# Attention and two feed-forward layers on one core: the last 64 keys of four heads as one unit of the attention

## The chip, the cores and the metric

One core of one Trainium2 chip runs the whole program in a single launch. The metric is the device time of one execution in microseconds; of several executions the median is given, so lower is better. A profile is one further execution with the hardware profiler on, and times inside it are counted from the start of its span.

## The reference

Four batches, twelve heads, 448 tokens, head size 64; all data is float32.

```python
S = q.shape[2]                                   # 448
scores = matmul(q, k.T) / sqrt(64) - log(S)
attn = 1 / (1 + exp(-scores))                    # a sigmoid: no sum over the keys
out = matmul(attn, v)                            # (4, 12, 448, 64)
x = out.transpose(0, 2, 1, 3).reshape(1792, 768)
h = x @ w_in;   g = s * relu(h)**2 + b;                   x = g @ w_out      # 768 -> 2048 -> 768
h = x @ w_in2;  g = max(h, 0) + alpha * min(h, 0);        y = g @ w_out2     # 768 -> 2048 -> 768
```

The weights come as float64 and are turned into float32 on the chip.

## The kernel before

**Two stages.** First the attention, then the two feed-forward layers, each in two passes over half of the tokens. The change touches the attention alone.

**The attention's tiling.** Two heads j = 0, 1 form a head pair, numbered q = 0 to 23. Their keys and queries lie one head on partitions 0 to 63 and the other on 64 to 127, in one tile of 128 x 896 (448 columns of keys, 448 of queries). The 448 keys are cut into chunks c = 0 to 3 of 128, 128, 128 and 64 keys. One chunk of one head pair is a unit; there are 24 x 4 = 96, numbered u in that order. The lists of the program below call the tiles `ga`, since all of the attention's buffers are carved out of tiles that the next stage uses for other things.

**One unit.** `emit_qk` (line 234) multiplies keys by queries. A matmul takes 64 rows of the array (the head size) and 64 of its columns (64 keys), so a chunk of 128 keys is four matmuls, one in each quarter of the array: rows by head j, columns by key half h. `emit_sig` (line 248) applies the sigmoid on ScalarE to both heads at once and writes to SBUF. `emit_av` (line 257) multiplies values by the result: rows are now the 64 keys of half h, columns the 64 outputs of head j, again four matmuls in four quarters; what the two halves give is summed up in two separate PSUM banks of the tile `av`. The last chunk has only half h = 0: two matmuls instead of four in each step, and a sigmoid over 64 partitions.

**The order of the work** is written out by hand (`manual_schedule`): step u issues the key-query matmuls of unit u, the value matmuls of unit u - 2, and the sigmoid of unit u. Each engine runs its own instructions in that order and waits on semaphores. Scores have two PSUM buffers, `av` has two, `sg` five in SBUF, keys-and-queries four, values four.

**Around it.** `emit_x` (line 274), in the step that issues a head pair's last value matmul, sums the two banks: a ScalarE copy of one, then a VectorE add of the other, then for batches 0 and 1 a split in two terms on VectorE, for batches 2 and 3 a store to DRAM (line 289). Sixteen times the first weights are converted from float64: `convert` (line 123), four VectorE operations, in the steps that `conv_step` (line 307) names; it reads a tile `r` that came by DMA (line 120; two buffers), and its result is stored (line 158).

**Transfers.** All are issued by SyncE, in order. In step 4q + 2 the keys, queries and values of head pair q + 3 are loaded (lines 226 and 232), so they stand in SyncE's queue behind whatever earlier steps left there: the store of the last conversion, which waits for VectorE, and the next load of `r`, which waits until the conversion has read its buffer.

Of the kernel before, what the change touches and what calls it, by code (L numbers as in the profile page):

```python
# [11 lines left out]
AF = mybir.ActivationFunctionType  # L12
# [4 lines left out]
P = 128  # L17
# [16 lines left out]
def tile_kernel(  # L34
# [14 lines left out]
    B, NPR, _, SKQ = kq.shape  # L49
    S = SKQ // 2  # L50
    NCH = vt.shape[4]
    D = vt.shape[5]
    NK = NPR
    DM = NK * P
    NFC = w_in1.shape[0]
    QKSCALE = 1.0 / math.sqrt(D)
# [1 line left out]
    T2 = 2 * S  # L58
    NCUT = len(OUT_CUTS)
    PER = NFC + NK * NCUT  # L60
    LAST = S - (NCH - 1) * P

    def pool(name, bufs, **kw):
        return ctx.enter_context(tc.tile_pool(name=name, bufs=bufs, **kw))
# [13 lines left out]
    def acc_tile(name):  # L78
        return ps.tile([P, 2, 512], F32, tag="acc", name=name)

    def av_tile(name):
        return ps_av.tile([P, 2, 512], F32, tag="av", name=name)

    def t_tile(name):
        return tp.tile([P, T2], F32, tag="t", name=name)
# [4 lines left out]
    def split(hi, lo, src, eng_hi):  # L90
        if eng_hi == "A":
            nc.scalar.copy(hi, src)  # L92
        else:
            nc.vector.tensor_copy(hi, src)  # L94
        nc.vector.tensor_tensor(out=lo, in0=src, in1=hi.bitcast(F32), op=ALU.subtract)  # L95

    bias_t = const.tile([P, 1], F32, name="bias_t")
# [25 lines left out]
    def convert(j, w, eng):  # L123

        n = units[j][1]
        v = r64.pop(j)[:, : 2 * n].rearrange("p (n t) -> p n t", t=2)
        lo, hi = v[:, :, 0], v[:, :, 1]
        a = cvp.tile([P, WMAX], U32, tag="cva", name="cva")[:, :n]
        u = w[:, :n].bitcast(U32)

        if eng == "A":
            nc.scalar.activation(a.bitcast(F32), hi.bitcast(F32), AF.Relu, scale=-(2.0**-80))  # L134
        else:
            nc.vector.tensor_scalar(
                out=a.bitcast(F32), in0=hi.bitcast(F32), scalar1=-(2.0**-80), scalar2=0.0,
                op0=ALU.mult, op1=ALU.max,
            )
        nc.vector.scalar_tensor_tensor(  # L140
            out=a.bitcast(F32), in0=hi.bitcast(F32), scalar=2.0**-112, in1=a.bitcast(F32),
            op0=ALU.mult, op1=ALU.max,
        )

        nc.vector.tensor_scalar(
            out=u, in0=lo, scalar1=2.0**-29, scalar2=7.0, op0=ALU.mult, op1=ALU.min
        )
        nc.vector.scalar_tensor_tensor(  # L148
            out=u, in0=a, scalar=3, in1=u,
            op0=ALU.logical_shift_left, op1=ALU.bitwise_or,  # L150
        )
        to_store.append((j, w))

    def store32():
        for j, w in to_store:
            n = units[j][1]
            w32[j] = dram.tile([P, n], F32, tag=f"w{j}", name=f"w{j}")
            nc.sync.dma_start(out=w32[j], in_=w[:, :n])
        to_store.clear()
# [10 lines left out]
    def split_unit(i):  # L170
        if i >= len(uses):
            return
        n = units[uses[i]][1]
        t = whlp.tile([P, 2, WMAX], F32R, tag="whl", name="whl")
        split(t[:, 0, :n], t[:, 1, :n], wraw.pop(i)[:, :n], "A")
        whl[i] = t
# [7 lines left out]
    def next64():  # L184
        if at64[0] < len(order64):
            load64(order64[at64[0]])
            at64[0] += 1
# [4 lines left out]
    def x_tile(kc):  # L192
        x[kc] = xp.tile([P, 2, 2, S], F32R, tag=f"x{kc}", name=f"x{kc}")
        return x[kc]

    def x_store(key, shape_cols, name):
        if key not in x_dram:
            x_dram[key] = dram.tile([P, 2, S], F32, tag=name, name=name)
        return x_dram[key]


    NU = B * NPR * NCH
    kqt, vtt, sct, sgt, avt = {}, {}, {}, {}, {}
    stores = []

# [5 lines left out]
    def buffer(what, cols):  # L211
        first, n = place[what]
        t = ga[first + taken[what] % n]
        taken[what] += 1
        return t[:, WMAX : WMAX + cols]

    def where(u):
        q, c = divmod(u, NCH)
        bb, pr = divmod(q, NPR)
        return q, bb, pr, c  # L220

    def load_kq(q):
        if q < B * NPR:
            bb, pr = divmod(q, NPR)
            kqt[q] = buffer("kq", SKQ)
            nc.sync.dma_start(out=kqt[q], in_=kq[bb, pr])

    def load_v(q):
        if q < B * NPR:
            bb, pr = divmod(q, NPR)  # L230
            vtt[q] = buffer("v", 2 * NCH * D).rearrange("p (j c d) -> p j c d", j=2, c=NCH)
            nc.sync.dma_start(out=vtt[q], in_=vt[bb, pr])

    def emit_qk(u):
        q, bb, pr, c = where(u)
        t = kqt[q]
        sc = acc_tile("sc")
        for h in range(2 if c < NCH - 1 else 1):
            for j in range(2):
                rows = slice(j * D, (j + 1) * D)  # L240
                keys = slice(c * P + h * D, c * P + (h + 1) * D)
                nc.tensor.matmul(  # L242
                    sc[h * D : (h + 1) * D, j, :S], t[rows, keys], t[rows, S:],
                    start=True, stop=True,
                )
        sct[u] = sc

    def emit_sig(u):
        c = u % NCH
        n = P if c < NCH - 1 else LAST  # L250
        sg = buffer("sg", T2).rearrange("p (j s) -> p j s", j=2)
        nc.scalar.activation(  # L252
            sg[:n], sct.pop(u)[:n, :, :S], AF.Sigmoid, bias=bias_t[:n, 0:1], scale=QKSCALE
        )
        sgt[u] = sg

    def emit_av(u):
        q, bb, pr, c = where(u)
        if c == 0:
            avt[q] = av_tile("av")  # L260
        sg = sgt.pop(u)

        for h in range(2 if c < NCH - 1 else 1):
            for j in range(2):
                keys = slice(h * D, (h + 1) * D)
                nc.tensor.matmul(  # L266
                    avt[q][j * D : (j + 1) * D, h, :S],
                    vtt[q][keys, j, c, :],
                    sg[keys, j, :],
                    start=(c == 0),  # L270
                    stop=(c == NCH - 1 - h),
                )

    def emit_x(q):
        bb, pr = divmod(q, NPR)
        av = avt.pop(q)
        t = t_tile("xo")[:, :S]
        nc.scalar.copy(t, av[:, 0, :S])  # L278
        nc.vector.tensor_tensor(out=t, in0=av[:, 1, :S], in1=t, op=ALU.add)  # L279
        if bb < 2:  # L280
            if bb == 0:
                x_tile(pr)
            split(x[pr][:, 1, bb], x[pr][:, 0, bb], t, "V")
        else:
            stores.append((x_store((0, 1, pr), S, f"xa{pr}")[:, bb - 2], t))

    def flush_stores():
        for dst, t in stores:
            nc.sync.dma_start(out=dst, in_=t)
        stores.clear()  # L290
# [13 lines left out]
    nc.sync.dma_start(out=b_t, in_=b.to_broadcast([P, 1]))  # L304
    nc.sync.dma_start(out=al_t, in_=alpha)
    next64()
    conv_step = {4 + (k * 88) // NFC: k for k in range(NFC)}
    for u in range(NU + 2):
        if u < NU:
            emit_qk(u)  # L310
        if u >= 2:
            emit_av(u - 2)
        if u < NU:
            emit_sig(u)
        flush_stores()
        store32()
        if u % NCH == 1 and u > NCH:
            emit_x(u // NCH - 1)
        if u % NCH == 2:
            load_kq(u // NCH + 3)  # L320
            load_v(u // NCH + 3)
        if u in conv_step:
            k = conv_step[u]
            w = ga[k][:, :WMAX]
            convert(k, w, "V")
            wraw[k] = w
            next64()
        if u == NU - 4:
            split_unit(0)
        if u == NU - 1:  # L330
            split_unit(1)
# [126 lines left out]
    for n, st in enumerate(steps):  # L458
        kind, m, p, c, cut = st
# [71 lines left out]
```

## Time and profile before

| what | value |
|---|---|
| median of 3 runs | 1100.8 us (1100.18 to 1102.32) |
| the profiled execution | 1100.52 us, of which its span is 1098.7 us |
| TensorE busy in the span | 1090.1 us (99%) |
| attention: first key-query matmul, first matmul of the next stage | 4.2 us, 150.98 us |
| attention: sigmoids | 96 in 147 us |
| the rest of the span | 151 us to the end, TensorE busy 943.3 of 947 us up to 1098 |

Read it from TensorE: it has no idle time that counts after the first 4.2 us, so what the attention costs is what TensorE's quarters are occupied with, unless somebody makes it wait. The start times of the sigmoids are the best ruler, since each follows its unit's key-query matmuls at once.

### The profile page before, as it was taken

What the parts mean: (1) busy time and instruction counts of PE and PEld (TensorE: products, weight loads), DVE (VectorE), ACT (ScalarE), POOL (GpSimd) and SP (SyncE); (2) the same over time, 40 slices, a digit from 0 to 9 for tenths busy, and PEclk for the clock granted to TensorE, in tenths of its full rate; (3) what the DMA queues carried; (4) which work ended last, traced back from release to release, by engine and by line L of the source; (5) the groups of instructions that cost most, each with busy time, mean ns of one, the idle gap of its engine ahead of it and who ended that gap; (6) DMA issues with size and microseconds to landing.
All of it is one profiled execution on the core that took longest, in us unless ns stands there. A gap on an engine that the chain in (4) does not pass through costs nothing.

```text
span 1098.7 us, 14184 instructions
## 1 busy us (share of the span) xinstructions
PE 1090.1 (99%) x5952; PEld 930.7 (85%) x5952; DVE 449.6 (41%) x567; ACT 433.9 (39%) x519; POOL 0.2 (0%) x4
## 2 busy tenths in 40 slices
PE   8999999999999999999999999999999999999998
PEld 3444469999999999999999999999999999999997
DVE  3664433346455144544333244375552234431110
ACT  6777753334333134342323244453331344431110
POOL 0000000000000000000000000000000000000000
PEclk9999999999999999999999999999999999999999
DMA  6878720004677433344565511146773111122210
GB/s 248 303 266 309 241 111 1 1 11 145 216 212 223 146 99 120 117 137 141 185 211 187 180 53 48 44 118 184 242 220 116 60 58 58 41 65 67 84 55 34
DMA packets 46864, 147.22 MB, mean 134 GB/s; under 512 B 5584, under 2 KB 7120, under 8 KB 46800
## 3 DMA queue, kind: packets, MB, share of 16 engines
q1 hardware_dynamic: 46800, 146.31, 40.9%
q8 instruction: 47, 0.77, 0.3%
q14 instruction: 17, 0.14, 0.0%
HBM read 107.36 MB, written 38.93 MB: 133 GB/s over the span
## 4 chain that ended last, share of the span: by engine, by line
PE 99%; DMA 0%; ACT 0%; issue 0%
PE hps L344 43%; PE ops L344 43%; PE sc L242 7%; PE av L266 7%; DMA ga<-in_kq 0%; ACT o L411 0%
## 5 line engine op out<-in xcount | busy, mean ns | idle before, releaser
L344 PE MATMUL hps<-x,whl 128*128 128x448 f32 x2304 | 474.6, 367 | 0.0
L344 PE MATMUL ops<-g,whl 128*128 128x448 f32 (+1 forms) x2304 | 469.9, 365 | 0.0
L344 PEld LDWEIGHTS hps<-x,whl 128*128 128x128 f32 x2304 | 432.5, 188 | 42.0 <-issue 0.7
L344 PEld LDWEIGHTS ops<-g,whl 128*128 128x128 f32 x2304 | 432.6, 188 | 36.6
L95 DVE TENSOR_TENSOR whl<-wraw,whl 128x768 fp32r<-128x768 f32 (+1 forms) x120 | 108.3, 902 | 272.4 <-ACT whl L92 272.4
L92 ACT CAST whl<-wraw 128x768 fp32r<-128x768 f32 (+1 forms) x120 | 94.5, 787 | 204.3 <-PE ops L344 186.7
L242 PE MATMUL sc<-ga 64*64 64x448 f32 x672 | 143.9, 555 | 4.2 <-DMA ga<-in_kq 4.2
L266 PE MATMUL av<-ga,ga 64*64 64x448 f32 x672 | 142.2, 540 | 0.0
L252 ACT ACTIVATE ga<-sc,bias_t 128x896 f32<-128x896 f32 x96 | 96.6, 1007 | 40.8 <-PE sc L242 28.9
L365 ACT ACTIVATE t<-hps 128x896 f32<-128x896 f32 x32 | 29.4, 918 | 145.1 <-PE hps L344 145.1
L95 DVE TENSOR_TENSOR g<-t,g 128x896 fp32r<-128x896 f32 x64 | 69.9, 1093 | 33.4 <-ACT g L92 32.3
L242 PEld LDWEIGHTS sc<-ga 64*64 64x64 f32 x672 | 44.6, 134 | 44.5 <-issue 34.8
L371 DVE SCALAR_TENSOR_TENSOR t<-n,nal_t,t 128x896 f32<-128x896 f32 x32 | 36.9, 1152 | 104.1 <-ACT n L370 104.1
L266 PEld LDWEIGHTS av<-ga,ga 64*64 64x64 f32 x672 | 44.9, 133 | 40.1 <-issue 39.3
L94 DVE CAST g<-t 128x896 fp32r<-128x896 f32 x32 | 20.1, 627 | 130.8 <-ACT t L366 130.8
L369 ACT ACTIVATE t<-hps 128x896 f32<-128x896 f32 x32 | 29.4, 918 | 93.1 <-PE hps L344 93.1
L140 DVE SCALAR_TENSOR_TENSOR cva<-r,cva 128x768 f32<-128x768 f32 (+1 forms) x68 | 61.7, 907 | 0.6
L92 ACT CAST g<-t 128x896 fp32r<-128x896 f32 x32 | 30.1, 942 | 39.0 <-DVE t L371 39.0
L134 ACT ACTIVATE cva<-r 128x768 f32<-128x768 f32 (+1 forms) x52 | 44.4, 853 | 0.0
L411 ACT COPY o<-ops 128x896 f32<-128x896 f32 x12 | 10.9, 907 | 70.8 <-PE ops L344 57.1
L279 DVE TENSOR_TENSOR xo<-av,xo 128x448 f32<-128x448 f32 x24 | 15.0, 625 | 57.4 <-ACT xo L278 57.3
L148 DVE SCALAR_TENSOR_TENSOR wraw<-cva,wraw 128x640 uint32<-128x640 uint32 (+1 forms) x36 | 31.3, 870 | 1.2
(26 smaller groups left out, 242.9 us busy)
## 6 DMA issues: line engine op xcount, KB each, us to landing
r<-in_w_in SPq DMA_DIRECT2D x32, 768.0 KB, 5.4
wraw<-w SPq DMA_DIRECT2D x60, 384.0 KB, 3.0
r<-in_w_out SPq DMA_DIRECT2D x24, 640.0 KB, 4.8
ga<-in_kq SPq DMA_DIRECT2D x24, 448.0 KB, 6.6
r<-in_w_out SPq DMA_DIRECT2D x12, 768.0 KB, 5.5
w<-wraw SPq DMA_DIRECT2D x24, 320.0 KB, 5.7
wraw<-w SPq DMA_DIRECT2D x24, 320.0 KB, 3.0
ga<-in_vt SPq DMA_DIRECT2D x24, 256.0 KB, 6.8
```

Of the source, the lines that this page charges most:

```text
L92: nc.scalar.copy(hi, src)
L95: nc.vector.tensor_tensor(out=lo, in0=src, in1=hi.bitcast(F32), op=ALU.subtract)
L134: nc.scalar.activation(a.bitcast(F32), hi.bitcast(F32), AF.Relu, scale=-(2.0**-80))
L140: nc.vector.scalar_tensor_tensor(out=a.bitcast(F32), in0=hi.bitcast(F32), scalar=2.0**-112, in1=a.bitcast(F32), op0=ALU.mult, op1=ALU.max,)
L148: nc.vector.scalar_tensor_tensor(out=u, in0=a, scalar=3, in1=u, op0=ALU.logical_shift_left, op1=ALU.bitwise_or,)
L242: nc.tensor.matmul(sc[h * D : (h + 1) * D, j, :S], t[rows, keys], t[rows, S:], start=True, stop=True,)
L252: nc.scalar.activation(sg[:n], sct.pop(u)[:n, :, :S], AF.Sigmoid, bias=bias_t[:n, 0:1], scale=QKSCALE)
L266: nc.tensor.matmul(avt[q][j * D : (j + 1) * D, h, :S], vtt[q][keys, j, c, :], sg[keys, j, :], start=(c == 0), stop=(c == NCH - 1 - h),)
L344: nc.tensor.matmul(dst[:, bk, :c], w[a], mv[m][bk][:, :c], start=first and k == 0, stop=last and k == 2,)
L365: nc.scalar.activation(t3, h, AF.Relu)
L369: nc.scalar.activation(t3, h, AF.Relu)
L371: nc.vector.scalar_tensor_tensor(out=t, in0=n, scalar=nal_t[:, fc : fc + 1], in1=t, op0=ALU.mult, op1=ALU.add)
```

## The change

The units get another order and another last chunk. Two head pairs q (even) and q + 1 now share it: the unit (q, 3) takes the last 64 keys of q in the columns h = 0 and the last 64 keys of q + 1 in the columns h = 1, and q + 1 itself has only chunks 0 to 2. So two head pairs are 4 + 3 = 7 units instead of 8, and there are 84 units, each with four matmuls per step and a sigmoid over 128 partitions. The values' tile holds the last 64 keys twice, on partitions 0 to 63 and 64 to 127 (it did before, the second copy unused), so the h = 1 matmuls of the shared unit read them from the partitions where they are. The sums of the odd pair begin in the shared unit for bank h = 1 and in its chunk 0 for bank h = 0. `emit_x`, the loads and the conversions keep their rules, counted in the new steps: a load of pair q + 3 in the step of (q, 2), the sixteen conversions spread over 76 steps instead of 88.

```diff
-    NU = B * NPR * NCH
+    order = []
+    for q in range(0, B * NPR, 2):
+        order += [(q, c) for c in range(NCH)] + [(q + 1, c) for c in range(NCH - 1)]
+    NU = len(order)
...
-    def where(u):
-        q, c = divmod(u, NCH)
-        bb, pr = divmod(q, NPR)
-        return q, bb, pr, c
+    def tiles(u):
+
+        q, c = order[u]
+        if c == NCH - 1:
+            return [(h, q + h, c * P) for h in range(2)]
+        return [(h, q, c * P + h * D) for h in range(2)]
...
     def emit_qk(u):
-        for h in range(2 if c < NCH - 1 else 1):
+        for h, q, k0 in tiles(u):
             for j in range(2):
                 rows = slice(j * D, (j + 1) * D)
-                keys = slice(c * P + h * D, c * P + (h + 1) * D)
                 nc.tensor.matmul(
-                    sc[h * D : (h + 1) * D, j, :S], t[rows, keys], t[rows, S:],
+                    sc[h * D : (h + 1) * D, j, :S],
+                    kqt[q][rows, k0 : k0 + D],
+                    kqt[q][rows, S:],
                     start=True, stop=True,
                 )
...
     def emit_av(u):
-        for h in range(2 if c < NCH - 1 else 1):
+        for h, q, _ in tiles(u):
+            if q not in avt:
+                avt[q] = av_tile("av")
+            first = c == (NCH - 1 if q % 2 and h else 0)
+            last = c == (NCH - 1 if not q % 2 and not h else NCH - 2)
...
-    conv_step = {4 + (k * 88) // NFC: k for k in range(NFC)}
+    conv_step = {4 + (k * (NU - 8)) // NFC: k for k in range(NFC)}
...
-        if u % NCH == 1 and u > NCH:
-            emit_x(u // NCH - 1)
-        if u % NCH == 2:
-            load_kq(u // NCH + 3)
-            load_v(u // NCH + 3)
+        if u >= 2:
+            q, c = order[u - 2]
+            if c == NCH - 1 - q % 2:
+                emit_x(q)
+        if u < NU and order[u][1] == 2:
+            load_kq(order[u][0] + 3)
+            load_v(order[u][0] + 3)
```

TensorE's instructions at the program's start. `sc` is a score tile, `av` a sum; `ga0` and `ga1` hold keys and queries of pairs 0 and 1, `ga9` and `ga10` their values, `ga4` to `ga8` the sigmoids' results; x4 counts the matmuls. Before:

```order
L242 MATMUL sc_138<-ga0_93 64x448 x4
L266 MATMUL av_143<-ga4_97,ga9_102 64x448 x4
L242 MATMUL sc_151<-ga0_93 64x448 x2
L266 MATMUL av_143<-ga5_98,ga9_102 64x448 x4
L242 MATMUL sc_159<-ga1_94 64x448 x4
L266 MATMUL av_143<-ga6_99,ga9_102 64x448 x4
L242 MATMUL sc_176<-ga1_94 64x448 x4
L266 MATMUL av_143<-ga7_100,ga9_102 64x448 x2
```

The same place with the change:

```order
L245 MATMUL sc_138<-ga0_93 64x448 x4
L271 MATMUL av_143<-ga4_97,ga9_102 64x448 x4
L245 MATMUL sc_151<-ga0_93 64x448 x2
L245 MATMUL sc_151<-ga1_94 64x448 x2
L271 MATMUL av_143<-ga5_98,ga9_102 64x448 x4
L245 MATMUL sc_161<-ga1_94 64x448 x4
L271 MATMUL av_143<-ga6_99,ga9_102 64x448 x4
L245 MATMUL sc_178<-ga1_94 64x448 x4
L271 MATMUL av_143<-ga7_100,ga9_102 64x448 x2
L271 MATMUL av_185<-ga7_100,ga10_103 64x448 x2
```

The two matmuls of pair 0's last chunk and two of pair 1's now fill one score tile, and the matmuls on pair 1's keys begin one step earlier, in the middle of a unit.

SyncE's queue where pair 20 is loaded (its keys and queries go to `ga0`, its values to `ga9`; `r64` is a float64 weight, `w12` a converted one, `xa` a store of a finished sum). Before:

```order
L226 DMA ga3_96<-in_kq 128x896
L232 DMA ga12_105<-in_vt 128x512
L289 DMA xa4_998<-xo_995 128x448
L226 DMA ga0_93<-in_kq 128x896
L232 DMA ga9_102<-in_vt 128x512
L120 DMA r64_1018<-in_w_in1 128x1536
L158 DMA w12_1028<-ga12_105 128x768
```

With the change:

```order
L232 DMA ga3_96<-in_kq 128x896
L238 DMA ga12_105<-in_vt 128x512
L119 DMA r64_993<-in_w_in1 128x1536
L293 DMA xa4_987<-xo_984 128x448
L157 DMA w12_1006<-ga12_105 128x768
L232 DMA ga0_93<-in_kq 128x896
L238 DMA ga9_102<-in_vt 128x512
```

The load of pair 20 stood ahead of the transfers that wait for a conversion and now stands behind them.

## Rows read from the trace of the kernel before

**Rows 1.** The page's head: span; engines' busy time; TensorE's granted clock in 40 slices.
```profile
span 1098.7 us, 14184 instructions
...
PE 1090.1 (99%) x5952; PEld 930.7 (85%) x5952; DVE 449.6 (41%) x567; ACT 433.9 (39%) x519; POOL 0.2 (0%) x4
...
PEclk9999999999999999999999999999999999999999
```

**Rows 2.** The page's chain that ended last: shares of the span by engine.
```profile
PE 99%; DMA 0%; ACT 0%; issue 0%
```

**Rows 3.** Groups by line and shape, first 170 us: busy us, mean ns | idle before.
```profile
L242 PE MATMUL sc<-ga 64*64 64x448 f32 x672 | 143.9, 555 | 4.2 <-DMA ga<-in_kq 4.2
L266 PE MATMUL av<-ga,ga 64*64 64x448 f32 x672 | 142.2, 540 | 0.0
L252 ACT ACTIVATE ga<-sc,bias_t 128x896 f32<-128x896 f32 x72 | 72.6, 1008 | 29.7 <-PE sc L242 17.8 <-PE av L266 10.0 <-ACT xo L278 0.4
...
L252 ACT ACTIVATE ga<-sc,bias_t 64x896 f32<-64x896 f32 x24 | 24.1, 1003 | 11.1 <-PE sc L242 11.1
...
L278 ACT COPY xo<-av 128x448 f32<-128x448 f32 x24 | 12.6, 523 | 0.5 <-PE av L266 0.5
```

**Rows 4.** ScalarE in order of time: units 0, 16, 18 to 20 and 95.
```profile
6.04 1.01 ACT L252 ACTIVATE ga<-sc,bias_t 128x896 f32<-128x896 f32 x1 [3.82 <-PE sc L242]
...
30.18 1.01 ACT L252 ACTIVATE ga<-sc,bias_t 128x896 f32<-128x896 f32 x1 [0.53 <-PE sc L242]
...
33.19 1.01 ACT L252 ACTIVATE ga<-sc,bias_t 128x896 f32<-128x896 f32 x1
34.66 1.00 ACT L252 ACTIVATE ga<-sc,bias_t 64x896 f32<-64x896 f32 x1 [0.46 <-PE sc L242]
36.19 1.01 ACT L252 ACTIVATE ga<-sc,bias_t 128x896 f32<-128x896 f32 x1 [0.53 <-PE sc L242]
...
148.91 1.00 ACT L252 ACTIVATE ga<-sc,bias_t 64x896 f32<-64x896 f32 x1 [0.46 <-PE sc L242]
```

**Rows 5.** TensorE in order of time: unit 20's eight key-query records, others left out.
```profile
34.44 0.55 PE L242 MATMUL sc<-ga 64*64 64x448 f32 x3
...
34.82 0.85 PE L242 MATMUL sc<-ga 64*64 64x448 f32 x4
...
35.51 0.54 PE L242 MATMUL sc<-ga 64*64 64x448 f32 x1
```

**Rows 6.** SyncE in order of time: loads of pair 5 and pair 23.
```profile
26.20 0.38 SPq L226 DMA_DIRECT2D ga<-in_kq  x1
...
131.95 0.33 SPq L120 DMA_DIRECT2D r<-in_w_out  x1
...
133.37 0.40 SPq L226 DMA_DIRECT2D ga<-in_kq  x1
```

**Rows 7.** Issue to landing (last number, us): loads of pairs 5, 16 and 23.
```profile
ga<-in_kq SPq DMA_DIRECT2D x1, 448.0 KB, 6.0
...
ga<-in_kq SPq DMA_DIRECT2D x1, 448.0 KB, 6.8
...
ga<-in_kq SPq DMA_DIRECT2D x1, 448.0 KB, 8.1
```

**Rows 8.** ScalarE in order of time: units 81 and 92.
```profile
127.90 1.01 ACT L252 ACTIVATE ga<-sc,bias_t 128x896 f32<-128x896 f32 x1 [0.50 <-PE sc L242]
...
144.43 1.01 ACT L252 ACTIVATE ga<-sc,bias_t 128x896 f32<-128x896 f32 x1 [0.53 <-PE sc L242]
```

**Rows 9.** DMA in the first 155 us; two windows (last: clock, DMA share, GB/s).
```profile
DMA packets 13983, 40.60 MB, mean 262 GB/s; under 512 B 1936, under 2 KB 3472, under 8 KB 13968
...
100.00:120.00 20.00, 20.00 (x192) 8.84 (x185) 9.50 (x15) 14.69 (x17) 0.00 (x0) 1.00 0.89 319
...
100.00:104.00 4.00, 4.00 (x44) 1.76 (x37) 2.79 (x4) 2.51 (x4) 0.00 (x0) 1.00 1.02 411
```

**Rows 10.** TensorE in order of time: the next stage's first matmuls.
```profile
150.98 5.33 PE L344 MATMUL hps<-x,whl 128*128 128x448 f32 x25
```

## What I predict

> **What bounds the kernel now.** I read the page's head first. TensorE is busy 99% of a span of 1098.7 us at the full granted clock (2.4 GHz of the two levels 1.2 and 2.4) [rows 1], and the chain that ended last is TensorE too, 99% [rows 2]. So time is gained only where TensorE is occupied for less long. The groups by line come next: in the attention the key-query matmuls waited once, 4.2 us at the start for the first load, and the value matmuls never [rows 3]. The two groups' busy times, 143.9 and 142.2 us, overlap almost fully: both run through the same stretch, in different quarters of the array. Hence a group's busy time can't be used as a cost, and a ruler is needed that counts each moment once.
>
> That ruler is the sigmoid, one per unit. Its starts run from 6.04 us (unit 0) to 148.91 us (unit 95) [rows 4]: 142.87 us over 95 steps, 1.504 us a step. The reader is to see that the half unit is not cheaper: unit 18 starts at 33.19, unit 19 (64 partitions, two matmuls instead of four) at 34.66, unit 20 at 36.19, steps of 1.47 and 1.53 us, and four units from 30.18 to 36.19 are 6.01 us [rows 4]. Three full steps and a half one take four full steps. The reason is in the layout: a quarter gets one key-query matmul and one value matmul per unit, and in a half unit the quarter of rows 0 and columns 0 still gets both, while the other quarters get one or none. The fullest quarter sets the pace.
>
> **What the change removes.** It removes 12 of 96 steps. The number of matmuls is the same (24 pairs x 14 of each kind), and each quarter now has the same number. 12 x 1.504 = 18.05 us. From the execution's own 1100.52 us that is 1082.5 us. That execution lies 0.28 us below the median of the runs shown and inside their spread of 2.1 us, so I keep its level. The bound on the shared unit's own step, which no row shows, is from both sides: 1.47 us (the half unit's step, though with half the matmuls) and 3.01 us, two steps (the halves run one after the other). I take 1.504 because it has exactly the four matmuls in four quarters of a full unit, and because the value matmuls of full units already stream four different operands into the four quarters at the pace of 1.504 us; that the two halves of the key-query step now stream different queries is therefore nothing new to the array. Should it behave like the half unit instead, another 0.03 us x 12 = 0.4 us is gained; more than that is excluded, since no quarter can do its two matmuls in less than the fullest quarter takes now.
>
> **What it adds on ScalarE and VectorE.** The sigmoid over 128 partitions takes 1008 ns, over 64 it took 1003 [rows 3]: nothing. ScalarE has per two pairs 7 x 1.008 + 2 x 0.523 = 8.1 us of work in 7 x 1.504 = 10.53 us; before it was 9.1 in 12.03. Its copy still ends ahead of the next sigmoid, as the step after a copy in the trace is no longer than others (30.18 to 36.19 contains one). The sum of a pair must be out of PSUM four steps (6.0 us) after `emit_x` is issued instead of five (7.5 us); against that stand the copy, 0.52 us, and an add that may be behind one conversion. I cost this at nothing; cover gone, it would cost the excess of that sum over 6 us, and I see none within 1.5 us.
>
> **What it moves: the loads' lead.** This is what is late next. A load of pair q + 3 is emitted in the step of (q, 2). Before, its first matmul came 10 steps later, 15.04 us. Now it is 8 steps, 12.03 us (for an odd pair the first use is the shared unit, for an even one there are 3 + 3 + 2 steps), so each load has 3.0 us less. SyncE is in order, so a load behind a conversion loses more. In the new order of steps a conversion falls into the same step as `emit_x`, with a load right behind, twice: step 8 (load of pair 5 in step 9) and step 61 (load of pair 20 in step 62). Behind a waiting key-query matmul on TensorE stand the value matmuls, and the whole stage with them, so such a wait counts in full.
> When is a load needed? Unit 20's first key-query record starts at 34.44 us [rows 5] and its sigmoid at 36.19 [rows 4]: 1.75 us ahead. The second half of the eight records lies between 34.82 and 35.51 [rows 5]; I take 1.25 us ahead.
> Pair 5: before, the same conversion stood in step 9 and the load was issued at 26.20 us [rows 6]; one step earlier is 24.70, and with the landing of 6.0 us [rows 7] the keys are there at 30.70. They are needed in the second half of unit 17: its sigmoid would start at 6.04 + 17 x 1.504 = 31.61, less 1.25 is 30.36. Wait: 0.3 us.
> Pair 20: the same figure of conversion, store and load stood before at pair 23. Unit 81's sigmoid started at 127.90 [rows 8], SyncE issued the weight load, freed by the conversion, at 131.95 and the pair's load at 133.37 [rows 6], 5.47 us after the sigmoid; it landed 8.1 us later [rows 7], at 141.47, and was needed at 144.43 [rows 8] - 1.75 = 142.68. It was 1.2 us early with 11 steps between conversion and use. Now there are 9 (61 to 70): 3.0 us less, 1.8 us late. With the landing of 6.8 us of pair 16 [rows 7], which was loaded behind a conversion too, it is 0.5 us late. Between the ends I take 1.1 us.
> The other loads follow a conversion that VectorE has done earlier, or none. Sum of waits 1.4 us, from 0 (both in time) to 3.5 us (both at the late end, and one more pair of their kind).
>
> **Sum.** 1100.52 - 18.05 + 1.4 = 1083.9 us. The feed-forward stage keeps its order and its work; it starts 16.65 us sooner.
>
> **The rivals.**
> *Transfers set the pace.* The first 155 us move 40.60 MB [rows 9]. Nearly all of it now falls into about 134 us: 303 GB/s instead of 262. In the second half, where finished sums are stored too, two pairs need, by the tiles' sizes, 2 x (448 + 256 + 224) KB and, with a conversion every 76 / 16 = 4.75 steps, 7 / 4.75 weights of 768 + 384 KB: 3.64 MB in 10.53 us, 346 GB/s. For it: the busiest 20 us already show a share of 0.89 at 319 GB/s [rows 9]. Against it: at a share of 1.02 there were 411 GB/s [rows 9], and the mean leaves gaps. If the 40.60 MB went at 319 GB/s and no faster, the last would land at 127 us, just ahead of the stage's end; at 300 GB/s at 135 us, which is 4 to 5 us on top: 1086 to 1093 us with queueing. Chance 0.11.
> The Trainium skill speaks against the change here: its page "DMA: Bandwidth & Descriptors", section "Where 436 GB/s comes from", says that transfers between HBM and SBUF are held by the HBM side at about 358 GB/s a core. By it the 3.64 MB would take 10.2 of 10.53 us, and by the row's 411 GB/s 8.9 us. The trace does not agree with the page as a ceiling; 4 us at 411 GB/s stand against it, so I don't raise the chance for it.
>
> *The change doesn't do what it says.* If the two heads' halves of a shared unit don't run beside each other, each shared step is two: 12 x 1.504 comes back, 1100.5 us; if only the key-query half is held up, half of it, 1091.5 us. Against it is the pace of the value matmuls above. Chance 0.05.
>
> *Slower: every load is late.* With four buffers and loads tied to steps, TensorE's step can't be shorter than an eighth of the time from a load's step to its landing. The latest in the trace is pair 23: step 82's first key-query record, 1.504 - 1.75 us from unit 81's sigmoid, is at 127.65, and the keys land at 141.47, 13.8 us later. If denser traffic made that the rule for all and added to it, the 84 steps would take 84 x T / 8; they are as long as before, and 2.2 us more, at T = 14.0 us. At T = 15 us they take 157.5 us, 13 more than 144.4: 1114 us. Against it: only loads that stand behind a conversion of the same step come near (pair 5: step 10 begins at 6.04 + 10 x 1.504 - 1.75 = 19.33, landing 32.2, 12.9 us), and there are now two such of 24. Chance 0.02.
>
> **Chances.** Forecast with its own range, 1082.2 to 1086: 0.80. Better than that: 0.02. Pace of transfers 0.11, halves one after the other 0.05, slower 0.02. The range is 1082.2 to 1087.5: below lies only 0.02, above it some 0.13. A change under 0.2% (2.2 us) can't be told from none by a measurement of this kernel. Faster is then all of the first three and about half of the fourth, 0.95; same 0.03; slower 0.02.
>
> **What would show it.** Right: 84 sigmoids over 128 partitions, 1.50 us apart through shared units as well; the next stage's first matmul near 134.3 us instead of 150.98 [rows 10]; waits of key-query matmuls for loads of pair 5 at about 30 us and pair 20 at about 110 us, together 1 to 2 us, none elsewhere; VectorE never waiting for a weight load after the first. Wrong: a step of 2 us or more around each shared unit (the halves don't overlap), a wait at most pairs (the transfers set the pace), ScalarE waiting for nothing while TensorE waits for a sigmoid (ScalarE has become the bound), or a granted clock below full anywhere.

## The result, and the profile after

The changed kernel takes 1083.71 us (median of 4 runs, 1081.99 to 1085.06) against 1100.49 us beside it: a ratio of 0.9844, 95% interval 0.9825 to 0.9863. Timed a second time, with the experiments, it took 1082.74 us (5 runs), ratio 0.9833 (0.9820 to 0.9847). The forecast was 1083.9 us. One execution of a later program, the one with the conversions five steps apart, took 2585.45 us, for a cause that nothing here shows, and stands in no ratio.

The changed kernel's page, its head, its chain, and the groups of the attention that answer to [rows 1 to 3]:

```profile
span 1081.5 us, 14147 instructions
...
PE 1073.0 (99%) x5952; PEld 945.9 (87%) x5952; DVE 449.6 (42%) x567; ACT 422.0 (39%) x507; POOL 0.2 (0%) x4
...
PE 99%; DMA 0%; ACT 0%; issue 0%
...
L245 PE MATMUL sc<-ga 64*64 64x448 f32 x672 | 108.9, 551 | 4.0 <-DMA ga<-in_kq 4.0
L271 PE MATMUL av<-ga,ga 64*64 64x448 f32 x672 | 107.1, 539 | 0.0
L255 ACT ACTIVATE ga<-sc,bias_t 128x896 f32<-128x896 f32 x84 | 84.6, 1008 | 35.5 <-PE sc L245 33.5
```

The span is 17.2 us shorter, TensorE is still busy 99% of it, and the number of matmul records is the same, 672 and 672; only the stretch in which they stand is shorter. The two groups' busy times fell by 35 us each, which shows once more that they can't be added.

ScalarE of the changed kernel in order of time, the stretch around the shared unit 31 (pairs 8 and 9) and around unit 17 (the first use of pair 5):

```profile
51.98 1.01 ACT L255 ACTIVATE ga<-sc,bias_t 128x896 f32<-128x896 f32 x1
53.48 1.01 ACT L255 ACTIVATE ga<-sc,bias_t 128x896 f32<-128x896 f32 x1 [0.50 <-PE sc L245]
54.99 1.01 ACT L255 ACTIVATE ga<-sc,bias_t 128x896 f32<-128x896 f32 x1 [0.50 <-PE sc L245]
```

```profile
30.43 1.01 ACT L255 ACTIVATE ga<-sc,bias_t 128x896 f32<-128x896 f32 x1
32.44 1.01 ACT L255 ACTIVATE ga<-sc,bias_t 128x896 f32<-128x896 f32 x1 [1.00 <-PE sc L245]
```

The shared unit starts at 53.48, 1.50 us after its neighbour and 1.51 ahead of the next: it costs what a full unit costs. At unit 17 the step is 2.01 us, 0.5 too long. Over the whole stage the sigmoids run from 5.86 to 131.66 us, 125.80 us over 83 steps. At 1.504 us that would be 124.8; the other 1.0 us are unit 17 and one step at the start (below). The next stage's first matmul, which answers to [rows 10]:

```profile
133.73 2.50 PE L350 MATMUL hps<-x,whl 128*128 128x448 f32 x11
```

150.98 to 133.73 us is 17.25 us, all of the span's difference: nothing was given back later.

### The profile page after: what moved, and what is told of

Its sections match the earlier page's. It is cut to its first block, busy times and chain, and to the rows that moved or that the text cites. A ratio compares the mean times of both kernels' runs of the same rounds, so it can differ in the third digit from the quotient of the medians.

```text
span 1081.5 us, 14147 instructions
## 1 busy us (share of the span) xinstructions
PE 1073.0 (99%) x5952; PEld 945.9 (87%) x5952; DVE 449.6 (42%) x567; ACT 422.0 (39%) x507; POOL 0.2 (0%) x4
## 4 chain that ended last, share of the span: by engine, by line
PE 99%; DMA 0%; ACT 0%; issue 0%
PE hps L350 44%; PE ops L350 43%; PE sc L245 6%; PE av L271 6%; DMA ga<-in_kq 0%; ACT o L417 0%
## 5 line engine op out<-in xcount | busy, mean ns | idle before, releaser
L245 PE MATMUL sc<-ga 64*64 64x448 f32 x672 | 108.9, 551 | 4.0 <-DMA ga<-in_kq 4.0
L271 PE MATMUL av<-ga,ga 64*64 64x448 f32 x672 | 107.1, 539 | 0.0
L255 ACT ACTIVATE ga<-sc,bias_t 128x896 f32<-128x896 f32 x84 | 84.6, 1008 | 35.5 <-PE sc L245 33.5
L271 PEld LDWEIGHTS av<-ga,ga 64*64 64x64 f32 x672 | 47.2, 134 | 23.4 <-issue 12.0
L245 PEld LDWEIGHTS sc<-ga 64*64 64x64 f32 x672 | 40.5, 136 | 28.9 <-issue 11.0
```

The source lines that it names most:

```text
L245: nc.tensor.matmul(sc[h * D : (h + 1) * D, j, :S], kqt[q][rows, k0 : k0 + D], kqt[q][rows, S:], start=True, stop=True,)
L255: nc.scalar.activation(sg, sct.pop(u)[:, :, :S], AF.Sigmoid, bias=bias_t[:, 0:1], scale=QKSCALE)
L271: nc.tensor.matmul(avt[q][j * D : (j + 1) * D, h, :S], vtt[q][keys, j, c, :], sg[keys, j, :], start=first, stop=last,)
```

## Experiments

**Is it the new order, or the array?** Both runs take each shared unit apart again into two half units, neighbours, 96 units in all. In the first both halves work in the columns h = 0, in the second the odd pair's half in the columns h = 1.

```diff
-        order += [(q, c) for c in range(NCH)] + [(q + 1, c) for c in range(NCH - 1)]
+        order += [(q, c) for c in range(NCH)] + [(q + 1, c) for c in (3, 0, 1, 2)]
...
         if c == NCH - 1:
-            return [(h, q + h, c * P) for h in range(2)]
+            return [(0, q, c * P)]          # first run
+            return [(q % 2, q, c * P)]      # second run
```

(The two runs' lines are put together here. The sigmoid's partitions follow, and in the first run the start flag.)

> The changed program, but each shared unit is taken apart into two half units, one behind the other, both in the columns h = 0 (96 units again, the two last chunks of a couple of pairs adjacent; the loads of odd pairs one step earlier than in the kernel before). Theory S (a unit costs one step of 1.504 us whatever it fills, and the gain is 12 steps): 1100 to 1101 us, the last sigmoid 142.9 us after the first. Rival O (the gain comes from the new order, the loads' and conversions' new places): stays near 1084 to 1090 us. Rival Q (only each quarter's sum of work counts): quarter of rows 0 and columns 0 has 96 units' work, so 1100 us as well.

Measured: 1100.42 us, ratio to the kernel before 0.9996 (0.9987 to 1.0005). The order gives nothing by itself; rival O is out.

> As the run with the units taken apart, but the odd pair's half unit works in the columns h = 1 and on the second copy of the values, as in the shared unit: the quarters' sums of work are those of the changed kernel, only the two halves are two units. Theory S (the array takes the units in order, a unit costs a step): 1100 to 1101 us. Rival Q (each quarter's sum of work counts, the array lets the second half run beside the first): 1083 to 1086 us, steps of under 0.3 us between the two half units' sigmoids or ScalarE as the new limit at about 1.0 us. Rival O: 1084 to 1090 us.

Measured: 1085.02 us, 0.9849 (0.9833 to 0.9864). Theory S fell, and rival Q holds: a unit of its own doesn't cost a step. ScalarE in order of time, first with both halves in the same columns, then in different ones; the half units are the rows of 64 partitions:

```profile
44.43 1.01 ACT L256 ACTIVATE ga<-sc,bias_t 128x896 f32<-128x896 f32 x1
46.19 1.00 ACT L256 ACTIVATE ga<-sc,bias_t 64x896 f32<-64x896 f32 x1 [0.76 <-PE sc L245]
47.40 1.00 ACT L256 ACTIVATE ga<-sc,bias_t 64x896 f32<-64x896 f32 x1 [0.20 <-PE sc L245]
48.94 1.01 ACT L256 ACTIVATE ga<-sc,bias_t 128x896 f32<-128x896 f32 x1 [0.54 <-PE sc L245]
```

```profile
40.24 1.01 ACT L256 ACTIVATE ga<-sc,bias_t 128x896 f32<-128x896 f32 x1
42.00 3.17 ACT L256 ACTIVATE ga<-sc,bias_t 64x896 f32<-64x896 f32 x3 [0.76 <-PE sc L245]
...
45.67 2.02 ACT L256 ACTIVATE ga<-sc,bias_t 128x896 f32<-128x896 f32 x2
```

In the same columns three steps from 44.43 to 48.94 take 4.51 us, 1.50 each. In different columns three sigmoids follow almost without a gap (two half units and, merged into the row, the next unit's): the three steps from 40.24 take some 3.9 us, and the second half's scores were ready before ScalarE was. TensorE itself, in order of time in the run with different columns:

```profile
40.48 0.54 PE L245 MATMUL sc<-ga 64*64 64x448 f32 x1
40.49 0.58 PE L272 MATMUL av<-ga,ga 64*64 64x448 f32 x1
40.70 0.54 PE L245 MATMUL sc<-ga 64*64 64x448 f32 x1
40.71 0.58 PE L272 MATMUL av<-ga,ga 64*64 64x448 f32 x1
40.85 0.54 PE L245 MATMUL sc<-ga 64*64 64x448 f32 x1
```

Key-query and value matmuls, which the program issues in blocks, start alternately: work in different quarters runs side by side across units. The Trainium skill's page "TensorE: Matmul & The Clock Gate", section "The mechanism", says that matmuls stay in program order; by it these blocks would not mix, and this trace does not agree.

**And without neighbours?** The kernel before, where only the odd pairs' half unit moves to the columns h = 1; order, loads and conversions stay.

```diff
-        for h in range(2 if c < NCH - 1 else 1):
+        for h in range(2) if c < NCH - 1 else [q % 2]:
```

(The key columns, the sigmoid's partitions and the stop flag follow.)

> The kernel before with one thing changed: the half unit of odd pairs works in the columns h = 1 and on the second copy of the values; order, 96 units, loads and conversions as before. No two half units are neighbours, they stand four units apart. Rival Q (each quarter's sum of work counts, and the array carries one quarter's lead through three full units): 1082 to 1086 us, steps after a half unit of odd and even pairs unlike. Theory L (the array makes up for idle quarters only between neighbours, since each full unit's scores and sigmoid need both halves and there are two score buffers): 1098 to 1101 us.

Measured: 1089.12 us, 0.9898 (0.9883 to 0.9913). In between, outside both ranges: two thirds of the gain. The array carries a lead over three full units, but not all of it. One line of who waited for whom between 5 and 145 us, in this run, in the changed kernel and in the run with half units in different columns (us in total, times, longest):

```profile
PEld sc L243 <- ACT ga L254: 7.6, 30, 1.1
```

```profile
PEld sc L245 <- ACT ga L255: 1.1, 1, 1.1
```

```profile
PEld sc L245 <- ACT ga L256: 13.0, 37, 1.1
```

TensorE's weight loads for the next scores waited 30 times, 7.6 us, for a sigmoid to free one of the two score buffers. That is about the difference to the changed kernel, some 6 us, but it is not shown to be its cause: the run with half units in different columns has more of the same wait, 13.0 us, and takes 1085.02 us. More score buffers were not tried, so where the last third of the gain goes stays open.

**Does the second half ride along free?**

```diff
-            return [(h, q + h, c * P) for h in range(2)]
+            return [(0, q, c * P)]
```

(The sigmoid's partitions and the start flag follow. The last 64 keys of the odd pairs are left out.)

> The changed program without the odd pair's half in the shared unit: the last 64 keys of the odd pairs are left out, so the shared unit has two matmuls instead of four in each step and a sigmoid over 64 partitions. Theory S (the second half rides along free): 1083.7 us within 1 us; without the odd pair's keys in the shared unit the wait at pair 5 (0.5 us) goes, so rather 1083.2. Rival H (the two halves hold each other up in part): shorter by 12 x the part, at 0.2 us each 2.4 us, 1081.3 us.

Measured: 1084.59 us (1083.44 to 1086.51), 0.9848. Leaving half of the shared work out gains nothing; rival H is out. Its profile held something else. ScalarE and TensorE around unit 70, the first of pair 20, and the issue-to-landing row of that pair's load:

```profile
110.02 1.01 ACT L256 ACTIVATE ga<-sc,bias_t 128x896 f32<-128x896 f32 x1
113.07 1.01 ACT L256 ACTIVATE ga<-sc,bias_t 128x896 f32<-128x896 f32 x1 [2.05 <-PE sc L245]
```

```profile
111.97 0.98 PE L245 MATMUL sc<-ga 64*64 64x448 f32 x8 [1.35 <-DMA ga<-in_kq]
```

```profile
ga<-in_kq SPq DMA_DIRECT2D x1, 448.0 KB, 8.3
```

This is the wait that was forecast for pair 20: landing after 8.3 us, a step of 3.05 us, 1.5 too long. In the changed kernel's profile the same row reads:

```profile
ga<-in_kq SPq DMA_DIRECT2D x1, 448.0 KB, 6.8
```

There unit 70's step was 1.50 us. The load stands at the same place in both queues; why it landed 1.5 us later in this execution was not found.

**Are the loads what is late?** Keys and queries of pair q + 3 are loaded in the step of (q, 0), ahead of the conversion.

```diff
-        if u < NU and order[u][1] == 2:
+        if u < NU and order[u][1] == 0:
             load_kq(order[u][0] + 3)
+        if u < NU and order[u][1] == 2:
             load_v(order[u][0] + 3)
```

> The changed program with the keys and queries of pair q + 3 loaded two steps earlier, in the step of (q, 0); the values stay where they were. Theory W (what the loads cost is their place behind a conversion): no wait for keys after the start, pair 5's 0.5 us gone, steps of 1.50 us throughout from the third on, time 1083.2 us, 0.5 below the changed kernel, which a time can't tell but the sigmoids can. Rival (the 0.5 us step at unit 17 is not the load): the long step stays.

Measured: 1082.40 us (1081.86 to 1082.95), 0.9825 (0.9810 to 0.9840). ScalarE at units 16 and 17:

```profile
30.63 1.01 ACT L255 ACTIVATE ga<-sc,bias_t 128x896 f32<-128x896 f32 x1
32.16 1.01 ACT L255 ACTIVATE ga<-sc,bias_t 128x896 f32<-128x896 f32 x1 [0.52 <-PE sc L245]
```

The step at unit 17 is 1.53 us: theory W holds for the place. The time was then compared on one chip with the changed kernel.

> The changed kernel once more, beside the one with early keys. If the load of pair 20 lands late by chance in some executions, this profile shows a step of 1.5 to 3.1 us at unit 70, and times between 1082 and 1086 us; else 1.50 us there.

> The changed kernel with keys and queries loaded two steps earlier, once more beside the changed kernel. Theory W: 0.5 to 1.5 us below it, 1082 to 1083 us, and a smaller spread, since no execution has a late load.

Measured: changed kernel 1082.74 us (1081.80 to 1083.12), early keys 1082.66 us (1082.09 to 1083.37). The gain of 0.5 to 1.5 us and the smaller spread that were expected of early keys did not come. In this profile of the changed kernel the load of pair 5 landed half a microsecond sooner and the step at unit 17 was 1.56 us; pair 20's landed after 6.9 us and the step at unit 70 was 1.58. So no version was found that beats the changed kernel clearly.

The other way of moving the conversions:

```diff
-    conv_step = {4 + (k * (NU - 8)) // NFC: k for k in range(NFC)}
+    conv_step = {4 + 5 * k: k for k in range(NFC)}
```

> The changed program with the sixteen conversions five steps apart (4, 9, ..., 79): the second conversion is in step 9 instead of 8 and the thirteenth in 64 instead of 61, so that the loads of pairs 5 and 20 stand ahead of them. Theory W: no long step at unit 17, none at unit 70, 1083.2 us. Rival (the load of pair 5 is late for want of lead alone): the long step at unit 17 stays.

Measured: 1083.36, 1084.03 and 1087.07 us, a ratio of 0.9853 (0.9825 to 0.9881). Unit 17 and unit 70 had ordinary steps, as expected, but long ones turned up elsewhere: 2.11 us at unit 73, 1.65 at units 28 and 38. Each is the first use of a pair whose load is issued in the step after a conversion (steps 64, 19 and 29). Half confirmed: what decides is who stands ahead of a load, and moving the conversions moves the queue to other pairs.

**What a late load costs, and how near the transfers are to their limit.**

```diff
-        if u < NU and order[u][1] == 2:
-            load_kq(order[u][0] + 3)
-            load_v(order[u][0] + 3)
+        if u < NU and order[u][1] == 2 and order[u][0] > 0:
+            load_kq(order[u][0] + 2)
+            load_v(order[u][0] + 2)
```

> The changed program with every load one pair later: in the step of (q, 2) pair q + 2 is loaded instead of q + 3. The lead falls from 8 steps (12.0 us) to 5 (7.5 us) for even pairs and 4 (6.0 us) for odd ones. Landing takes 6 to 8 us from issue. Theory W1 (a wait for keys counts in full): odd pairs wait 0.5 to 2 us each, 11 of them, and those behind a conversion 4 to 6 us: 1095 to 1115 us. Theory W2 (lateness up to 0.5 us is swallowed, since key-query and value matmuls can trade places): about 0.5 us less at each late pair, 1090 to 1110 us; small waits without a longer step between sigmoids should be seen.

Measured: 1112.02 us, 1.0093 (1.0068 to 1.0118), slower than the kernel before. TensorE's waits for keys, at the matmuls and at the weight loads (us in total, times, longest; the first row holds the 4.1 us at the start too), two of them in order of time, and three windows (us, busy time of TensorE, of its weight loads, VectorE, ScalarE, GpSimd, granted clock, DMA share, GB/s):

```profile
PE sc L245 <- DMA ga<-in_kq: 20.7, 10, 4.7
PEld sc L245 <- DMA ga<-in_kq: 16.5, 7, 5.4
```

```profile
30.06 0.98 PE L245 MATMUL sc<-ga 64*64 64x448 f32 x8 [2.77 <-DMA ga<-in_kq]
121.38 1.01 PE L245 MATMUL sc<-ga 64*64 64x448 f32 x2 [4.66 <-DMA ga<-in_kq]
```

```profile
31.40:34.70 3.30, 3.30 (x23) 1.29 (x17) 0.00 (x0) 1.75 (x2) 0.00 (x0) 0.50 0.74 228
100.00:120.00 20.00, 16.00 (x160) 7.17 (x152) 10.11 (x15) 11.44 (x14) 0.00 (x0) 1.00 0.80 256
120.20:126.80 6.60, 5.42 (x32) 2.06 (x35) 0.00 (x0) 1.57 (x2) 0.00 (x0) 0.50 0.95 380
```

The loss of some 29 us against the changed kernel is made of waits and of what goes with them: in the wait of 4.66 us the granted clock fell to 0.50, TensorE's 1.2 GHz level, and stood there from 120.20 to 126.80 us, and matmul records took about twice as long (1.01 us against 0.54). W1's range (1095 to 1115 us) holds the time, W2's (1090 to 1110) ends 2 us below it; but neither counted the lower clock, so the time doesn't tell them apart. It does show the "slower" rival's mechanism at work, at a lead of 4 to 5 steps; at the change's 8 it doesn't appear.

```diff
             load_v(order[u][0] + 3)
+            q = order[u][0]
+            more = dram.tile([P, SKQ], F32, tag=f"more{q}", name=f"more{q}")
+            nc.sync.dma_start(out=more, in_=kq[q // NPR, q % NPR])
```

> The changed program with one more transfer of 448 KB per pair, from DRAM to DRAM, behind the pair's loads; nothing reads it. 11 MB more are read and written in the attention. Theory D (the transfers are near their limit after the change): loads land later, 5 us or more lost, 1089 us and up, with waits at many pairs. Theory S (the transfers have room): under 3 us, 1084 to 1087 us.

Measured: 1085.28 us, 0.9858 (0.9836 to 0.9881), 1.6 to 2.5 us above the two timings of the changed kernel. One window of the run with more traffic, then the busiest of the changed kernel:

```profile
40.00:60.00 20.00, 20.00 (x218) 10.67 (x215) 15.20 (x24) 14.90 (x18) 0.00 (x0) 1.00 1.03 415
```

```profile
80.00:100.00 20.00, 20.00 (x218) 14.62 (x214) 7.82 (x11) 14.82 (x18) 0.00 (x0) 1.00 0.94 337
```

The changed kernel's 337 GB/s are not a limit: with 415 moved TensorE was still busy all of those 20 us. Long steps appeared only at the pairs that stand behind a conversion (unit 17 2.78 us, unit 70 3.15, unit 80 2.08); together they are 3.5 us too long, against 0.5 in the changed kernel. Theory D, with waits at many pairs, is out.

## Why the prediction was right

**The step and its count** were right. Twelve steps of 1.504 us fewer, 18.05 us, and the shared unit at 1.50 us, near the lower of the bounds 1.47 and 3.01, where the forecast took it. The prediction's reason, the fullest quarter sets the pace, is what the runs with the units taken apart show: two half units in the same quarters cost 1100.42 us, in different ones 1085.02, though the number of units is the same. In the experiments' expectations I had sharpened this to "a unit costs a step whatever it fills"; that fell. Sharing one score tile is not what gains most; it spares ScalarE one sigmoid of two.

**The waits** for loads, forecast as 1.4 us (1 to 2 us among the signs of being right), were 0.5 in the profiled execution; another 0.5 us came at the start, from something that was not in the sum. So part of the nearness of 1083.9 to 1083.71 us is luck, and the four executions lie 3 us apart.

| term | forecast | measured |
|---|---|---|
| 12 steps fewer | -18.05 | -18.05 (83 steps of 1.504) |
| pair 5, unit 17 | +0.3 | +0.5 |
| pair 20, unit 70 | +1.1 (0.5 to 1.8) | 0 here, 0.1 in the second profile, 1.5 in another program's execution |
| half rate at the start | none | +0.5 |
| first load's landing | none | -0.2 |
| span | -16.65 | -17.2 |

*Pair 5* was the right place: issued at 24.9 us where 24.70 was forecast, it landed after 6.4 us instead of 6.0.

*Pair 20* failed at two steps. One is the 1.75 us between a unit's first key-query record and its sigmoid, from which the prediction took when the keys are needed: that is read from the kernel before, where some quarters run ahead of others. In the changed kernel, with all quarters equally filled, they run level. Unit 16, ahead of any wait, has its eight records in one block, 1.06 us ahead of its sigmoid at 30.43:

```profile
29.37 0.92 PE L245 MATMUL sc<-ga 64*64 64x448 f32 x8
```

So keys are needed some 0.7 us later than was forecast, and that alone takes the lower end of the forecast wait, 0.5 us for a landing of 6.8 us, to nothing. The other step is the sentence that such a wait "counts in full". The load was issued at 104.04 us (forecast 103.55, from 6.04 + 61 x 1.504 + 5.47 and the 0.3 of pair 5) and landed after 6.8 us. TensorE's first records of unit 69 and the block of unit 70, and the sigmoids of the two units:

```profile
109.05 0.54 PE L245 MATMUL sc<-ga 64*64 64x448 f32 x2
...
110.99 1.02 PE L245 MATMUL sc<-ga 64*64 64x448 f32 x8
```

```profile
110.61 1.01 ACT L255 ACTIVATE ga<-sc,bias_t 128x896 f32<-128x896 f32 x1
112.11 1.01 ACT L255 ACTIVATE ga<-sc,bias_t 128x896 f32<-128x896 f32 x1 [0.50 <-PE sc L245]
```

One step after 109.05 is 110.55, so half of the records started 0.4 us later than their pace, and the sigmoid still came after 1.50 us: after unit 17 half of the quarters ran half a microsecond behind the others, so keys that came 0.4 us late held up quarters that had that much to spare. This is read from the records, not shown by an experiment of its own. At 8.3 us of landing the wait counted.

*The start* was not in the sum. TensorE's weight loads in order of time, in the kernel before and in the changed one:

```profile
8.73 0.23 PEld L266 LDWEIGHTS av<-ga,ga 64*64 64x64 f32 x4 [0.50 <-issue]
9.20 0.14 PEld L242 LDWEIGHTS sc<-ga 64*64 64x64 f32 x2 [0.23 <-issue]
```

```profile
9.30 0.25 PEld L245 LDWEIGHTS sc<-ga 64*64 64x64 f32 x4 [0.50 <-issue]
9.83 0.14 PEld L245 LDWEIGHTS sc<-ga 64*64 64x64 f32 x4 [0.28 <-issue]
```

A group of loads with the idle time ahead of it takes 0.73 to 0.75 us at first and about half of that later (0.23 + 0.14 = 0.37 us in the kernel before), and the step to it comes at about 9 us before and past 9.3 us after. The profile's windows give a granted clock of 1.00 in this stretch too, so what halves the pace is not shown. In the ten other profiles of this study it lies between 7.3 and 9.7 us whatever the program, so I put the 0.5 us down to the execution, not to the change.

**The rivals.** Transfers as the pace: the share rose as worked out (0.81 to 0.94 in windows of 20 us, at most 337 GB/s where 346 were worked out) but nothing waited for bandwidth, and 415 GB/s were moved with more traffic. Halves one after the other: excluded by 1.50 us. All loads late: needs a lead half as long.

## What to carry to other kernels

When small matmuls fill only quarters of the array, add up the work of each quarter: the fullest one is the price, and pieces that use the empty quarters come free if they stand next to each other and the engine behind them keeps up; four units apart they gave back two thirds. Count the steps with a ruler that counts each moment once (here the sigmoids), not the matmuls' busy times, which overlap. When a stage is made shorter, work out for every prefetch what its lead becomes in microseconds and what it stands behind in its queue, and give the price as a range, since landing times differ between executions. Read when the data is needed from the order that the change makes, not from the one that it replaces.

## What was not expected of the hardware

Matmuls of different instructions, issued in blocks, overlapped across units where their quarters differ, enough to hide twelve half units (1085.02 against 1100.42 us). In the run with late loads a wait of TensorE of 4.66 us went with a granted clock of 0.50 from 120.20 to 126.80 us, and after one of 2.77 us matmuls went on at 30.06 us and the clock stood at 0.50 from 31.40 to 34.70, while a wait of 1.35 us, in the run without the second halves, was followed by matmuls at the usual pace (the row at 111.97 us: 0.98 us for a block of eight).
